# Early k of batch 1, four more bias pieces on GpSimd, 16-row transfers in the last bias block, slots of 112 tokens

## The chip, the cores and the metric

The kernel runs on one core of one Trainium2 chip. The metric is the device time of one execution in microseconds (us). A run of it gives one time; the number quoted is the median of the runs shown. Beside that stands one profiled execution with a trace of every engine: TensorE (PE, and PEld for its weight loads), VectorE (DVE), ScalarE (ACT), GpSimd (POOL), SyncE (SP), and the transfers (DMA).

## What is computed

Three stages, one behind the other.

```python
# 1. attention, B=2, H=8, S=576, D=64, with an additive bias from a small MLP on relative position
scores = q @ k.T / sqrt(D)
x = log1p(abs(i - j)) / log1p(max(i, 1))
bias = relu(x * w1 + b1) @ w2              # 32 hidden values, one bias per head
attn = softmax(scores + bias)
x = attn @ v                               # to (1152, 512)
# 2. dense experts: E=4, every token goes through all, F=1024
out = sum_e p[:, e] * (relu(x @ w1[e]) @ w2[e])
# 3. routed experts: E=8, F=1024, every token goes to the one with the largest gate logit
e_idx = argmax(x @ w_gate)
out[mask_e] = gate_w * eom[:, e] * (relu(x[mask_e] @ w1[e]) @ w2[e])
```

With the reference's inputs the eight routed experts get 204, 48, 336, 0, 274, 21, 0 and 269 of the 1152 tokens.

## The kernel before, in words

**Attention.** The queries are cut into nine units of 128 rows: blocks 0 to 3 of 128 positions each for both batches, and a last unit with the 64 remaining positions of both. A unit has eight heads, so there are 72 steps n. A loop (L584) carries them as a pipeline: in round n TensorE makes scores of step n+3 (`qk`, L352), VectorE adds the bias and takes the maximum of step n+2 (`soft_max`, L361), ScalarE makes the exponentials of step n+1 (`soft_exp`, L371), and TensorE transposes step n and multiplies step n-2 by v (`av`, L411 to L413).

**The bias.** A block of 128 positions is made in eight groups T of sixteen positions: four pieces tt hold four positions each with the 32 hidden values on the partitions. `bias_r` (L297) makes one piece, relu of a slice of the table lm plus a column, on VectorE (L305), GpSimd (L308) or ScalarE (L310). `bias_mm` (L323) multiplies the four pieces by w2 into PSUM, `bias_out` (L332) scales them with ScalarE into a tile bo of 128 partitions (16 positions by 8 heads), and a transfer on SyncE's queue (L335) spreads it as 16 partitions by 8 by 576 into the block's bias tile, which `soft_max` reads. Which slice of lm is read follows from `row0` (L66). The last block, blk 4, has 64 positions, and its four groups issue four transfers of 8 partitions each (L339). The table lm has 1152 columns for all groups, with a step of 8 positions between the four partition groups, and is scaled by w1 once (L549 for its first 448 columns).

**The order of the work** is written out by hand; each engine takes its instructions in that order, and so does each DMA queue. Ahead of the loop stands a prologue (L514 to L583). SyncE's queue there carries lm's last 704 columns, q of unit 0 (`load_q`, L139), k of batch 0 (`load_k`, L184 and L188: two transfers of 256 positions and one of 64), then rounds T=0 to 10 with the eight bias groups of block 0 and two of the next block, and behind each group an entry of the list `bulk` (L539): k of batch 1, the first 448 columns of lm (`load_lm`, L537), three pieces of v of batch 0 (`load_v`, L230 and L233) and q of unit 1. The two halves of a transposed q (`q_trans`, L159; its copies between partitions L173 and L174) stand on the same queue.

In the loop the bias groups of the next block are made two pieces a round. RP and RE say which engine takes a piece:

```python
RP = 10
RE = ("vavv", "pavv")
...
bias_r(g[0], T, 2 * o + x, RE[n >= RP][2 * o + x])
```

So up to round 9 GpSimd takes none, and from then on one of four. GpSimd's in-order queue further holds the splits of q into a high and a low part (`split`, L146 and L147), and in round 4 the split of v of batch 1 (`v_hi` L271, `v_lo` L286 and L290), which waits for VectorE's scaling of v (L264).

**Dense experts.** 96 rounds i with two layers (L729 to L731 and L746 to L748); SyncE and GpSimd bring the weights, which ScalarE, VectorE and GpSimd split into pairs of f16; the routed experts' weights go back to memory as wdr.

**Routed experts.** Every token is given a rank within its expert (`rank`, L850). 128 tokens of an expert form a slot; slot number and place in it come from the rank's high and low bits. Three early slots (NE) are filled from the first 768 tokens, and NFIX = 13 slots are run in a pipeline; slots beyond the thirteenth run one after another behind an If on the count. For a slot, `ids_in` gathers its tokens' rows, `x_tr` (L1036) transposes them by four matmuls, `load_e` brings the expert's weights in eight transfers of 512 KB (four of them for each layer; skipped where the expert is that of the slots before), `lay1` (L1048) makes 96 matmuls with the weights stationary and the slot's 128 tokens moving, `lay2` (L1067) makes 24 with the tokens stationary and 512 columns moving, and L1072 writes the rows out. `step(s)` puts lay1 of slot s+1, x_tr of slot s+2 and lay2 of slot s behind one another.

## Time and profile before

| what | us |
|---|---|
| median of 3 runs (805.65 to 805.75) | 805.67 |
| the profiled execution | 805.57 |
| its span | 803.8 |
| PE busy | 746.6 (93%) |
| PEld busy | 479.8 (60%) |
| DVE busy | 489.1 (61%) |
| ACT busy | 476.7 (59%) |
| POOL busy | 352.2 (44%) |
| HBM read, written | 116.35 MB, 39.34 MB |

The span runs from the first to the last instruction of the profiled execution; the rest of its time lies around it. Busy time is the time in which an engine worked at something; the share is an average over stages that have different limits, so an engine with 60% can still be the one that is waited for in one stage. Matmuls are pipelined, so the rows of single ones overlap. In rows of waits the engine and tile that waited come first, then what ended the wait.

### The profile page before, as it was taken

Reading aid. Unit: us, or ns where it says so; the run is one execution under the profiler, and the core shown is the slowest. Engines: PE = TensorE matmul, PEld = TensorE weight load, DVE = VectorE, ACT = ScalarE, POOL = GpSimd, SP = SyncE. Lnnn points to the kernel's source line nnn. Section 1 sums busy time; section 2 is a strip of 40 time slices with the busy share of each in tenths; the row PEclk is TensorE's granted clock in tenths of the full one; section 3 lists DMA queues with packets and bytes.
Section 4 is the critical chain, followed back from the end, with each engine's and each line's share of the span. In section 5 each row is a group of like instructions: output and inputs, shape, how many; then the busy total and the mean of one; then the engine's idle time right before and its main releaser. Section 6 shows DMA issues by size and latency. Waiting matters only on the chain. (4 is left out here: it accounts for less than half of the span.)

```text
span 803.8 us, 16406 instructions
## 1 busy us (share of the span) xinstructions
PE 746.6 (93%) x6303; PEld 479.8 (60%) x6303; DVE 489.1 (61%) x1210; ACT 476.7 (59%) x694; POOL 352.2 (44%) x258
## 2 busy tenths in 40 slices
PE   6677999998889999999999999999998989999994
PEld 3255777776875554555555555555555577767771
DVE  6679999998787446555566465465567563333310
ACT  5577899996845757676676667667663122232220
POOL 8534644551643546555545555554533212211110
PEclk9979999999999999999999999999999999999998
DMA  7944344466255475556657467573526689998330
GB/s 178 207 94 100 91 108 101 126 177 131 69 196 209 152 285 198 206 221 254 235 188 263 166 246 279 195 261 130 211 108 256 204 307 386 409 407 327 131 142 17
DMA packets 73868, 160.21 MB, mean 199 GB/s; under 512 B 18936, under 2 KB 27640, under 8 KB 73786
## 3 DMA queue, kind: packets, MB, share of 16 engines
q1 hardware_dynamic: 67912, 144.38, 53.2%
q0 software_dynamic: 4528, 14.47, 5.3%
q8 instruction: 51, 0.84, 0.4%
q10 hardware_dynamic: 1346, 0.28, 0.2%
q14 instruction: 31, 0.25, 0.1%
HBM read 116.35 MB, written 39.34 MB: 194 GB/s over the span
## 5 line engine op out<-in xcount | busy, mean ns | idle before, releaser
L511 POOL TENSOR_TENSOR ring<-wraw,ring 128x1024 f16<-128x1024 f32 x64 | 136.2, 2130 | 118.8 <-ACT wraw L508 100.4
L734 DVE SCALAR_TENSOR_TENSOR h<-hps,h 128x384 f16<-128x384 f32 x96 | 53.2, 557 | 146.8 <-ACT h L733 146.8
L729 PE MATMUL hps<-xt,wt 128*128 128x384 f16 x384 | 125.9, 328 | 2.3 <-DVE h L734 1.8
L731 PE MATMUL hps<-xt,wt 128*128 128x384 f16 x384 | 126.0, 328 | 0.0
L730 PE MATMUL hps<-xt,wt 128*128 128x384 f16 x384 | 126.0, 328 | 0.0
L476 DVE TENSOR_REDUCE wm<-wraw 128x1 f32<-128x1024 f32 x96 | 116.0, 1209 | 0.0
L508 ACT ACTIVATE wraw<-wraw,wR 128x1024 f32<-128x1024 f32 x91 | 104.5, 1149 | 3.0
L746 PE MATMUL yps<-wt,h 128*128 128x512 f16 x264 | 100.1, 379 | 0.0
L747 PE MATMUL yps<-wt,h 128*128 128x512 f16 x264 | 100.1, 379 | 0.0
L748 PE MATMUL yps<-wt,h 128*128 128x512 f16 x264 | 100.1, 379 | 0.0
L733 ACT ACTIVATE h<-hps 128x384 f16<-128x384 f32 x96 | 46.7, 487 | 88.9 <-PE hps L731 84.8
L511 POOL TENSOR_TENSOR wt<-wraw,wt 128x1024 f16<-128x1024 f32 x31 | 66.1, 2134 | 63.2 <-ACT wraw L508 62.9
L503 ACT ACTIVATE ring<-wraw,wR 128x1024 f16<-128x1024 f32 x64 | 73.0, 1141 | 21.5 <-DVE wR L492 18.8
L1048 PE MATMUL l<-xb,wb 128*128 128x128 f16 x1248 | 73.7, 219 | 0.6 <-issue 0.2
L1048 PEld LDWEIGHTS <-wb 128*128 128x128 f16 x1248 | 71.0, 98 | 4.7 <-issue 1.6
L1067 PE MATMUL l<-wb,xb 128*128 128x512 f16 x312 | 69.5, 379 | 0.8 <-ACT o L1071 0.8
L352 PE MATMUL sc<-kt,qt 128*128 128x288 f32 x320 | 62.1, 319 | 7.8 <-DVE mn L361 6.0
L361 DVE CUSTOM_DVE_ANT_0 ns<-sc,bias 128x576 f32<-128x576 f32 x72 | 54.3, 754 | 21.7 <-PE sc L352 9.6
L305 DVE TENSOR_SCALAR_CACHE_REDUCE r<-lm,nbp 128x576 f32<-128x576 f32 x88 | 67.1, 807 | 0.2
L1056 DVE SCALAR_TENSOR_TENSOR xb<-l,xb 128x512 f16<-128x512 f32 x26 | 17.6, 691 | 80.6 <-ACT xb L1055 80.6
L1072 POOL DMA_INDIRECT out_x<-o,g x13 | 13.3, 1020 | 107.3 <-ACT o L1071 93.5
L371 ACT ACTIVATE e<-ns,mn 128x576 f32<-128x576 f32 x72 | 56.4, 784 | 1.9 <-DVE mn L361 1.7
(248 smaller groups left out, 1426.0 us busy)
## 6 DMA issues: line engine op xcount, KB each, us to landing
wb<-wdr SPq DMA_DIRECT2D x104, 512.0 KB
wraw<-in_moe_w SPq DMA_DIRECT2D x84, 512.0 KB
wdr<-ring SPq DMA_DIRECT2D x64, 512.0 KB
bias<-bo SPq DMA_DIRECT2D x32, 288.0 KB
wraw<-in_moe_w POOLq DMA_DIRECT2D x12, 512.0 KB, 5.0
qt<-qt SPq DMA_DIRECT2D x40, 128.0 KB
ydr<-y POOLq DMA_DIRECT2D x9, 258.0 KB, 3.4
bias<-bo SPq DMA_DIRECT2D x16, 144.0 KB
```

Source lines behind the costliest of these rows:

```text
L476: dve.tensor_reduce(out=wm[:, w_col(x), k:k + 1], in_=wraw[x][:, k], axis=AX.X, op=ALU.max, apply_absolute_value=True)
L503: act.activation(out=hi, in_=t, func=AF.Copy, scale=R)
L508: act.activation(out=t, in_=t, func=AF.Copy, scale=R)
L511: pool.tensor_tensor(out=lo, in0=t, in1=hi, op=ALU.subtract)
L729: pe.matmul(ps, lhsT=w[:, k, 0, fs], rhs=xt[:, c, 0, k, :], start=(k == 0), stop=False)
L730: pe.matmul(ps, lhsT=w[:, k, 0, fs], rhs=xt[:, c, 1, k, :], start=False, stop=False)
L731: pe.matmul(ps, lhsT=w[:, k, 1, fs], rhs=xt[:, c, 0, k, :], start=False, stop=(k == 3))
L746: pe.matmul(acc[m][t], lhsT=hh, rhs=w[:, f // 2, 0, ws], start=(f == 0), stop=False)
L747: pe.matmul(acc[m][t], lhsT=hh, rhs=w[:, f // 2, 1, ws], start=False, stop=False)
L748: pe.matmul(acc[m][t], lhsT=hl, rhs=w[:, f // 2, 0, ws], start=False, stop=(f == 7))
L1048: pe.matmul(ps[f // 4][:, f % 4, :], lhsT=w[:, k, a, f * 128:f * 128 + 128], rhs=xs[:, b, k, :], start=(k == 0 and f % 4 == 0 and i == 0), ...
L1067: pe.matmul(ps, lhsT=hs[:, a, f, :], rhs=w[:, f // 2, b, c], start=(f == 0 and i == 0), stop=(f == 7 and i == 2))
```

## The change

1. The three transfers of k of batch 1 stand right behind those of batch 0, ahead of the first bias group. `bulk` holds v of batch 0 in three pieces behind groups 0 to 2 and lm's first columns behind group 3; nothing stands behind the groups after that, and q of unit 1 is loaded behind the prologue's loop. The scaling of lm's first 448 columns goes from VectorE to ScalarE.
2. RP is 0: from round 0 on GpSimd takes one bias piece of four. That is one piece each in rounds 0, 2, 4, 6 and 8, which VectorE had.
3. In the last bias block the positions of a group are laid out so that two transfers of 16 partitions take the place of four of 8. This needs the table with a step of 4 between partition groups: a new tile lm4 of 128 x 640, loaded in round 22 and scaled by GpSimd in round 36.
4. A slot holds SL = 112 tokens. The rank is divided by 112 by a product and a shift; `x_tr`, `lay1`, `lay2` and the output take 112 rows or columns. The gather still brings 128 rows, and the tiles keep their size. The number of slots provided for is 21.

The diff without its unchanged lines:

```diff
@@ -42,18 +42,19 @@
-C_N = C_PERM + 16
+C_N = C_PERM + 20
...
-NSLOT = 19
+NSLOT = 21
+SL = 112
...
-RP = 10
+RP = 0
@@ -64,7 +65,7 @@
-    return blk * 128 + T + 32 * tt if blk < 4 else 512 + 2 * T + tt // 2 + 32 * (tt % 2)
+    return blk * 128 + T + 32 * tt if blk < 4 else 512 + T + 16 * tt
...
@@ -300,7 +302,7 @@
-        src = lm[:, 575 - r0:1151 - r0]
+        src = lm[:, 575 - r0:1151 - r0] if blk < 4 else lm4[:, 575 - r0:1151 - r0]
@@ -334,9 +336,8 @@
-        for x in range(2):
-            for p0 in (0, 64):
-                sp.dma_start(out=bias_t[blk][p0 + 2 * T + x:p0 + 64:8], in_=bo[64 * x:64 * x + 64])
+        for p0 in (0, 64):
+            sp.dma_start(out=bias_t[blk][p0 + T:p0 + 64:4], in_=bo)
@@ -516,6 +517,8 @@
+        for a in (2, 0, 1):
+            load_k(1, a)
@@ -536,8 +539,7 @@
-        bulk = [[lambda: load_k(1, 2), lambda: load_k(1, 0)], [lambda: load_k(1, 1)], [load_lm], [lambda: load_v(0, 0)],
-                [lambda: load_v(0, 1)], [lambda: load_v(0, 2)], [], [lambda: load_q(1)]]
+        bulk = [[lambda: load_v(0, 0)], [lambda: load_v(0, 1)], [lambda: load_v(0, 2)], [load_lm]]
@@ -546,7 +548,7 @@
-                dve.tensor_scalar(out=lm[:, 0:448], in0=lm[:, 0:448], scalar1=w1c, scalar2=None, op0=ALU.mult)
+                act.activation(out=lm[:, 0:448], in_=lm[:, 0:448], func=AF.Copy, scale=w1c)
@@ -563,6 +565,7 @@
+        load_q(1)
@@ -677,6 +680,10 @@
+            if n == 22:
+                sp.dma_start(out=lm4, in_=lmc[:, 1152:1792])
+            if n == 36:
+                pool.tensor_tensor(out=lm4, in0=lm4, in1=w1c.to_broadcast([128, 640]), op=ALU.mult)
@@ -861,10 +868,10 @@
-            dve.tensor_copy(rki[:, uu], rks[:, uu])
-            dve.tensor_scalar(out=rki[:, uu], in0=rki[:, uu], scalar1=127, scalar2=None, op0=ALU.bitwise_and)
-            dve.tensor_copy(lo7[:, uu], rki[:, uu])
-            dve.tensor_tensor(out=hi7[:, uu], in0=rks[:, uu], in1=lo7[:, uu], op=ALU.subtract)
+            dve.tensor_scalar(out=rki[:, uu], in0=rks[:, uu], scalar1=9363.0, scalar2=None, op0=ALU.mult)
+            dve.tensor_scalar(out=rki[:, uu], in0=rki[:, uu], scalar1=20, scalar2=None, op0=ALU.arith_shift_right)
+            dve.tensor_copy(hi7[:, uu], rki[:, uu])
+            dve.scalar_tensor_tensor(out=lo7[:, uu], in0=hi7[:, uu], scalar=-float(SL), in1=rks[:, uu], op0=ALU.mult, op1=ALU.add)
...
@@ -952,8 +959,8 @@
-        dve.tensor_scalar(out=ci, in0=pn[0:8, 0:1], scalar1=127.0, scalar2=None, op0=ALU.add)
-        dve.tensor_scalar(out=ci, in0=ci, scalar1=7, scalar2=None, op0=ALU.arith_shift_right)
+        dve.tensor_scalar(out=ci, in0=pn[0:8, 0:1], scalar1=SL - 1.0, scalar2=9363.0, op0=ALU.add, op1=ALU.mult)
+        dve.tensor_scalar(out=ci, in0=ci, scalar1=20, scalar2=None, op0=ALU.arith_shift_right)
...
@@ -1033,10 +1040,10 @@
-            pe.transpose(ps[:, a, :], xq[:, a * 128:a * 128 + 128], idn)
+            pe.transpose(ps[:, a, 0:SL], xq[0:SL, a * 128:a * 128 + 128], idn[0:SL, 0:SL])
...
-        act.copy(xs[:, 0], ps)
-        dve.tensor_tensor(out=xs[:, 1], in0=ps, in1=xs[:, 0], op=ALU.subtract)
+        act.copy(xs[:, 0, :, 0:SL], ps[:, :, 0:SL])
+        dve.tensor_tensor(out=xs[:, 1, :, 0:SL], in0=ps[:, :, 0:SL], in1=xs[:, 0, :, 0:SL], op=ALU.subtract)
@@ -1045,15 +1052,16 @@
-                    pe.matmul(ps[f // 4][:, f % 4, :], lhsT=w[:, k, a, f * 128:f * 128 + 128], rhs=xs[:, b, k, :],
+                    pe.matmul(ps[f // 4][:, f % 4, 0:SL], lhsT=w[:, k, a, f * 128:f * 128 + 128], rhs=xs[:, b, k, 0:SL],
...
-            act.activation(out=hs[:, 0, c], in_=ps[z], func=AF.Relu)
-            dve.scalar_tensor_tensor(out=hs[:, 1, c], in0=ps[z], scalar=0.0, in1=hs[:, 0, c], op0=ALU.max, op1=ALU.subtract)
+            act.activation(out=hs[:, 0, c, 0:SL], in_=ps[z][:, :, 0:SL], func=AF.Relu)
+            dve.scalar_tensor_tensor(out=hs[:, 1, c, 0:SL], in0=ps[z][:, :, 0:SL], scalar=0.0, in1=hs[:, 0, c, 0:SL], op0=ALU.max,
+                                     op1=ALU.subtract)
@@ -1064,12 +1072,12 @@
-                pe.matmul(ps, lhsT=hs[:, a, f, :], rhs=w[:, f // 2, b, c], start=(f == 0 and i == 0), stop=(f == 7 and i == 2))
+                pe.matmul(ps[0:SL], lhsT=hs[:, a, f, 0:SL], rhs=w[:, f // 2, b, c], start=(f == 0 and i == 0), stop=(f == 7 and i == 2))
...
-        act.activation(out=o, in_=ps, func=AF.Copy, scale=gs)
-        pool.indirect_dma_start(out=out, out_offset=bass.IndirectOffsetOnAxis(ap=ids, axis=0), in_=o, in_offset=None,
+        act.activation(out=o[0:SL], in_=ps[0:SL], func=AF.Copy, scale=gs[0:SL])
+        pool.indirect_dma_start(out=out, out_offset=bass.IndirectOffsetOnAxis(ap=ids[0:SL], axis=0), in_=o[0:SL], in_offset=None,
@@ -1245,7 +1253,7 @@
-    at = np.array([[row0(t // 32, t // 4 % 8, t % 4) + 8 * g for t in range(144)] for g in range(4)])
+    at = np.array([[row0(t // 32, t // 4 % 8, t % 4) + (8 if t < 128 else 4) * g for t in range(144)] for g in range(4)])
@@ -1276,8 +1284,9 @@
-    g = 8 * np.repeat(np.arange(4), 32)[:, None]
-    lm = np.log1p(np.abs(np.arange(1152)[None, :] - 575 - g).astype(np.float32))
+    g = np.repeat(np.arange(4), 32)[:, None]
+    x = np.arange(1792)[None, :]
+    lm = np.log1p(np.abs(np.where(x < 1152, x - 575 - 8 * g, x - 1152 - 575 - 4 * g)).astype(np.float32))
```

How the order of the instructions moves, at three places.

SyncE's queue at the start, before (kraw and ks are k, vraw is v, bias the bias tile, qt a transposed q):

```order
L188 DMA kraw_128<-in_k 128x8x128 x2
L184 DMA ks<-in_k 64x8x64
L335 DMA bias_164<-bo 16x8x576
L184 DMA ks<-in_k 64x8x64
L188 DMA kraw_190<-in_k 128x8x128
L173 DMA qt<-qt 64x512
L174 DMA qt<-qt 64x512
L335 DMA bias_164<-bo 16x8x576
L188 DMA kraw_190<-in_k 128x8x128
L335 DMA bias_164<-bo 16x8x576
L537 DMA lm<-in_lmc 128x448
L335 DMA bias_164<-bo 16x8x576
```

The same queue from the same place in the change:

```order
L190 DMA kraw_129<-in_k 128x8x128 x2
L186 DMA ks<-in_k 64x8x64 x2
L190 DMA kraw_136<-in_k 128x8x128 x2
L337 DMA bias_170<-bo 16x8x576
L232 DMA vraw<-in_v 128x4x128 x2
L175 DMA qt<-qt 64x512
L176 DMA qt<-qt 64x512
L337 DMA bias_170<-bo 16x8x576
L232 DMA vraw<-in_v 128x4x128 x2
L337 DMA bias_170<-bo 16x8x576
L235 DMA vraw<-in_v 64x4x64 x2
L337 DMA bias_170<-bo 16x8x576
```

All of k now stands ahead of the first bias group, and the transfers between the groups are those of v; lm's first columns follow the fourth group instead of the third.

GpSimd's queue from the split of q of unit 1 (qs) on, before; v and vz are v of batch 1, r a bias piece:

```order
L146 TENSOR_TENSOR qs<-q,one 128x8x64
L147 TENSOR_TENSOR qs<-q,qs 128x8x64
L271 TENSOR_TENSOR v<-vraw,one 128x8x64
L286 TENSOR_TENSOR v<-vraw,v 128x8x64
L271 TENSOR_TENSOR v<-vraw,one 128x8x64
```

In the change:

```order
L148 TENSOR_TENSOR qs<-q,one 128x8x64
L149 TENSOR_TENSOR qs<-q,qs 128x8x64
L310 TENSOR_SCALAR r<-lm,nbp 128x576 x3
L273 TENSOR_TENSOR v<-vraw,one 128x8x64
L288 TENSOR_TENSOR v<-vraw,v 128x8x64
```

Three bias pieces now stand ahead of the split of v. GpSimd's queue at the end of that split, before:

```order
L286 TENSOR_TENSOR v<-vraw,v 128x8x64
L271 TENSOR_TENSOR vz<-vraw,one 64x4x64 x2
L290 TENSOR_TENSOR vz<-vraw,vz 64x4x64 x2
L146 TENSOR_TENSOR qs<-q,one 128x8x64
L147 TENSOR_TENSOR qs<-q,qs 128x8x64
L308 TENSOR_SCALAR r<-lm,nbp 128x576 x4
```

In the change:

```order
L288 TENSOR_TENSOR v<-vraw,v 128x8x64
L273 TENSOR_TENSOR vz<-vraw,one 64x4x64 x2
L292 TENSOR_TENSOR vz<-vraw,vz 64x4x64 x2
L310 TENSOR_SCALAR r<-lm,nbp 128x576 x2
L148 TENSOR_TENSOR qs<-q,one 128x8x64
L149 TENSOR_TENSOR qs<-q,qs 128x8x64
L310 TENSOR_SCALAR r<-lm,nbp 128x576 x4
```

Two bias pieces now stand between the split of v and the next split of q.

ScalarE's queue near the end of the prologue (r a bias piece, bo a bias group out of PSUM, kt a part of k), before:

```order
L217 CAST kt_120<-ktp 128x4x64 x2
L310 ACTIVATE r<-lm,bps 128x576
L332 ACTIVATE bo<-bp,bconst,cs 128x288 x2
L310 ACTIVATE r<-lm,bps 128x576
L332 ACTIVATE bo<-bp,bconst,cs 128x288 x2
L310 ACTIVATE r<-lm,bps 128x576
L332 ACTIVATE bo<-bp,bconst,cs 128x288 x4
```

In the change:

```order
L219 CAST kt_121<-ktp 128x4x64 x2
L312 ACTIVATE r<-lm,bps 128x576
L551 ACTIVATE lm<-lm,cs 128x448
L334 ACTIVATE bo<-bp,bconst,cs 128x288 x2
L312 ACTIVATE r<-lm,bps 128x576
L334 ACTIVATE bo<-bp,bconst,cs 128x288 x2
L312 ACTIVATE r<-lm,bps 128x576
```

The scaling of lm stands between the piece of round 7 and the copies of group 6.

## Rows read from the trace of the kernel before

**Rows 1.** Windows of the prologue; the columns are in the first line.
```profile
core 0: us, PE busy (x) PEld busy (x) DVE busy (x) ACT busy (x) POOL busy (x), PEclk, DMA share, GB/s
2.00:9.00 7.00, 1.98 (x8) 0.86 (x8) 3.15 (x10) 2.35 (x6) 5.17 (x8) 1.00 1.09 275
9.00:13.00 4.00, 4.00 (x24) 1.84 (x26) 4.00 (x13) 1.90 (x4) 3.84 (x5) 1.00 0.02 2
...
20.00:28.00 8.00, 7.04 (x73) 3.91 (x71) 7.22 (x20) 7.67 (x17) 7.73 (x7) 1.00 1.14 215
28.00:36.00 8.00, 4.11 (x47) 1.30 (x48) 5.97 (x13) 4.11 (x8) 3.70 (x3) 1.00 1.16 214
36.00:42.00 6.00, 1.04 (x16) 0.57 (x8) 0.00 (x0) 0.99 (x3) 0.00 (x0) 0.60 1.04 168
```

**Rows 2.** Timeline of the prologue: start, duration, engine, line, tiles, wait before.
```profile
28.09 1.48 DVE L549 TENSOR_SCALAR lm<-lm,cs 128x448 f32<-128x448 f32 x1 [0.87 <-DMA lm<-in_lmc]
29.67 0.78 ACT L310 ACTIVATE r<-lm,bps 128x576 f32<-128x576 f32 x1 [1.03 <-DVE lm L549]
...
41.01 1.07 ACT L332 ACTIVATE bo<-bp,bconst,cs 128x288 f32<-128x288 f32 x2 [5.35 <-DMA bias<-bo]
42.49 0.76 DVE L361 CUSTOM_DVE_ANT_0 ns<-sc,bias 128x576 f32<-128x576 f32 x1 [8.30 <-DMA bias<-bo]
```

**Rows 3.** The page's DMA issues: size of one, us to landing.
```profile
ydr<-y POOLq DMA_DIRECT2D x9, 258.0 KB, 3.4
```

**Rows 4.** The page's costliest groups: VectorE's bias pieces, busy and mean ns.
```profile
L305 DVE TENSOR_SCALAR_CACHE_REDUCE r<-lm,nbp 128x576 f32<-128x576 f32 x88 | 67.1, 807 | 0.2
```

**Rows 5.** Timeline of GpSimd and TensorE from 71 to 87 us.
```profile
71.42 1.04 POOL L271 TENSOR_TENSOR v<-vraw,one 128x512 f16<-128x512 f32 x1 [12.00 <-DVE vraw L264]
...
81.65 1.39 POOL L290 TENSOR_TENSOR vz<-vraw,vz 64x256 f16<-64x256 f32 x2
...
85.49 1.74 POOL L308 TENSOR_SCALAR r<-lm,nbp 128x576 f32<-128x576 f32 x1
80.75 1.18 PE L323 MATMUL bp<-r,cs 128*32 128x288 f32 x16
85.57 0.66 PE L159 MATMUL qtp<-cs,qs 128*128 128x128 f32 x4 [0.72 <-POOL qs L147]
```

**Rows 6.** A window inside the last bias block's transfers.
```profile
190.00:193.00 3.00, 2.86 (x38) 2.50 (x35) 2.91 (x6) 2.91 (x6) 0.00 (x0) 1.00 0.53 125
```

**Rows 7.** Waits from 176 to 205 us: total, times, longest.
```profile
ACT bo L332 <- issue: 2.6, 1, 2.6
DVE ns L361 <- PE sc L352: 2.4, 2, 2.2
...
ACT bo L332 <- DMA bias<-bo: 1.3, 1, 1.3
```

**Rows 8.** Waits from 100 to 150 us.
```profile
POOL r L308 <- PE bp L323: 24.3, 10, 3.3
```

**Rows 9.** Timeline of TensorE in the routed experts.
```profile
732.52 5.77 PE L1048 MATMUL l<-xb,wb 128*128 128x128 f16 x96
...
754.92 5.52 PE L1048 MATMUL l<-xb,wb 128*128 128x128 f16 x96
...
760.72 5.34 PE L1067 MATMUL l<-wb,xb 128*128 128x512 f16 x24
```

**Rows 10.** Timeline of TensorE and its weight loads in the attention, near 62 us.
```profile
61.76 0.20 PE L411 MATMUL avp<-v,eth 128*128 128x65 f16 x1
...
62.05 0.19 PE L411 MATMUL avp<-v,eth 128*128 128x65 f16 x1
61.80 0.10 PEld L413 LDWEIGHTS <-etl 128*128 128x128 f16 x1
```

**Rows 11.** The page's DMA issues: the routed experts' weights.
```profile
wb<-wdr SPq DMA_DIRECT2D x104, 512.0 KB
```

**Rows 12.** Windows in the routed experts.
```profile
730.00:735.00 5.00, 5.00 (x58) 3.59 (x57) 0.77 (x5) 1.30 (x2) 1.05 (x1) 1.00 1.03 410
...
740.00:745.00 5.00, 5.00 (x42) 2.92 (x40) 1.93 (x8) 1.00 (x2) 0.03 (x1) 1.00 0.03 7
...
760.00:765.00 5.00, 5.00 (x32) 2.65 (x30) 3.58 (x10) 1.54 (x3) 0.00 (x0) 1.00 1.03 419
```

More of the change, by code (lines that the diff above doesn't have):

```diff
@@ L125, in attn_moe_moe_kernel @@
     lm = lm_p.tile([128, 1152], F32, name="lm")
+    lm4 = lm_p.tile([128, 640], F32, name="lm4")
     nbp = lm_p.tile([128, 144], F32, name="nbp")
@@ L940, in bump @@
         bm = rt_p.tile([1, 8], F32, name="bm")
-        dve.tensor_scalar(out=bm, in0=pb, scalar1=-1.0, scalar2=128.0, op0=ALU.mult, op1=ALU.add)
+        dve.tensor_scalar(out=bm, in0=pb, scalar1=-1.0, scalar2=float(SL), op0=ALU.mult, op1=ALU.add)
         dve.scalar_tensor_tensor(out=bm, in0=bm, scalar=0.0, in1=oh2[0:1, :], op0=ALU.max, op1=ALU.mult)
@@ L970, in slot_table @@
         dve.tensor_reduce(out=st1, in_=st8, axis=AX.X, op=ALU.add)
-        dve.scalar_tensor_tensor(out=st1, in0=hi7, scalar=1.0 / 128, in1=st1, op0=ALU.mult, op1=ALU.add)
+        dve.tensor_tensor(out=st1, in0=hi7, in1=st1, op=ALU.add)
         dve.tensor_tensor(out=nl, in0=cs[:, C_PERM:C_PERM + NLATE].unsqueeze(1).to_broadcast([128, NU, NLATE]),
```

## The prediction, made before the changed kernel was run

> **What bounds the kernel now.** I read the page's busy shares and its 40 slices first: TensorE is busy 93% of the span, so time can be won only where it is not full or where its own work shrinks. Two such places are the first slices and the expert stage. I then read a table of windows over the first 42 us, the timeline there, and the same two views where each part of the change lands.
>
> In the first 42 us the transfers set the pace. They run at 275 GB/s to 9 us, then the DMA engines stand idle for 4 us (share 0.02) and from 13 us on they are full at about 215 GB/s, while TensorE's work thins out [rows 1]. The timeline shows who waits: the first block of lm lands at 28.09, the last bias copies of ScalarE stand 5.35 us behind earlier bias transfers, and the first addition of scores and bias on VectorE starts at 42.49 after 8.30 us of waiting for a bias transfer [rows 2]. Around 80 us GpSimd's queue is the tight one, near 190 us the bias transfers of the last block, and in the expert stage TensorE and the weight loads alternate; their rows come with the terms.
>
> **The prologue.** The 1.18 MB of k of batch 1 (8x576x64 floats) leave the crowded stretch for the idle one: at 275 GB/s they take 4.3 us, from 9 to 13.3 us [rows 1]. What then has to pass before batch 0's first block can be added to is eight bias groups of 0.295 MB, v of batch 0 (1.18), four halves of q transposed (0.52) and the first part of lm (0.23): 4.29 MB. At 215 GB/s they end at 33.3; I add 3.4 us from issue to landing, the row of a 258 KB transfer [rows 3], so the first addition starts near 37 instead of 42.49. I round the gain to **-5.2**, since ScalarE now scales the 448 columns of lm (about 0.6 us, from its 0.78 for 576 columns) where VectorE took 1.48, and that stands on the chain to the last groups [rows 2]. The ends: the gain can't exceed the wait of 8.30, and if the last stretch's 168 GB/s (it goes with a granted clock of 0.60, the 1.2 GHz level for part of it, after TensorE had done little) holds for all 4.29 MB, they end at 38.8 and -3.7 is left. That lm is queued behind v now costs nothing by itself: v was on the same queue ahead of the last groups before. The q load that moves behind the loop was ahead of nothing that this wait needs.
>
> **GpSimd's queue.** With RP=0 five bias pieces move from VectorE (807 ns each [rows 4]) to GpSimd (1.74 us each [rows 5]). Three of them stand ahead of the split of v of batch 1 and fit into the 12.00 us that GpSimd idles there. The other two stand behind it. The split runs from 71.42 to 83.04; if VectorE's relief lets it start 0.8 us earlier, the piece of n=6 ends at 83.04 - 0.8 + 1.74 = 84.0, while the bias matmul that reads it ran at 80.75 [rows 5]: TensorE's in-order queue stands 3.2 us later there. The second piece and the split of the next q follow on GpSimd, 2 x 1.74 - 0.8 = 2.7 later, and the transposes of that q at 85.57 had already waited 0.72 for GpSimd [rows 5]; most of it lies in the same delay. Afterwards TensorE is full, so a shift stays: **+2.8**. The ends: +1.6, if three pieces less on VectorE (2.4 us) bring the split forward by all of that, and +5.5, if the second delay comes on top of the first. The saved 5 x 0.81 us of VectorE give nothing else where TensorE is full. Further pieces alternate as before.
>
> **The last bias block.** Its transfers were four of 8 partitions for each group; now two of 16. While they run, the DMA share is 0.53 at 125 GB/s [rows 6], against 1.16 at 214 with 16-partition transfers [rows 1]. ScalarE's copies wait 1.3 and 2.6 us there and VectorE's additions wait 2.4 in two places for scores that TensorE issues later [rows 7]. I take the 2.4 that reach the chain, **-2.4**; the ends are 0 (ScalarE has slack enough) and -3.9 (both copies' waits). The new table lm4 costs a load of 320 KB, under 2 us of a queue that is not full, and one scaling on GpSimd, about 1.3 us by columns (1.74 for 576 [rows 5]); between pieces GpSimd waits 24.3 us in ten waits for TensorE [rows 8], which hides it. Without that cover it would cost its 1.3 us.
>
> **The expert stage.** A slot has 96 matmuls whose moving side shrinks from 128 to 112 columns. At 128 they take 5.52 us, 57.5 ns each [rows 9]; nine of 64 or 65 columns start within 0.29 us, 32 ns apart [rows 10]. 63 columns are thus worth about 25 ns, 16 columns 6.3 ns, a slot **0.60 us**, and its four transposes at most 0.06 more. The 24 matmuls of the second layer keep 512 moving columns and their 5.34 us [rows 9].
> The Trainium skill ("TensorE: Matmul & The Clock Gate", section "Back-to-back issue gap") says that in a stream of weight load and matmul pairs the spacing is set by both, and gives 81 ns at 128 columns; by that the narrower slot would gain little. The trace disagrees on the figure (57.5 ns).
> The thirteen slots do not all profit. Two steps take 22.40 us from one first layer to the one two slots later, 11.2 each [rows 9]. Eight weight transfers of 512 KB a slot [rows 11] at 410 GB/s take 10.2 us [rows 12], and with gather and output some 0.5 MB more, 11.4. So up to about 740 us transfers run without pause and a faster TensorE only meets its weights sooner; at 740 to 745 they pause (share 0.03) because slots 9 and 10 keep the weights of slot 8, and they run again at 760 [rows 12]. I give the nine slots before 2.5 us together (the slack that their weights have) and the last four 4 x 0.66 = 2.7: **-5.2**. The ends: -3.5 (only the last four and part of the routing) and -8.5 (thirteen slots, and 0.4 around the routing). The routing replaces four small VectorE instructions by four; one load of 20 instead of 16 constants and longer tables weigh nothing beside this.
>
> **Sum.** -5.2 + 2.8 - 2.4 - 5.2 = -10.0 against the profiled execution's 805.57 (span 803.8): 795.6. The median of the runs shown is 805.67, 0.1 above it, so **795.7 us** as a median. A measurement of this kernel can tell a change of about 0.2% (1.6 us) from none.
>
> **The rivals.**
> A, the forecast, 0.57; its own range 793 to 798.5.
> B, GpSimd's queue is dearer and the prologue gives least: -3.7 + 5.5 - 2.4 - 5.2 = -5.8, **799.9**. For it speaks that after a thin stretch the granted clock was 0.60 [rows 1], so that a wait is paid in slower matmuls too; against it that GpSimd idled 12 us just before. 0.14.
> C, weights are not what limits the slots and all thirteen gain 0.62: -8.1 in place of -5.2, **792.8**. For it: the first-layer rows lie within 0.25 us of each other whether the DMA is full or not [rows 9, 12]. Against it: 11.4 us of transfers in a step of 11.2. 0.13.
> D, the first layer is paced by its 96 weight loads rather than by columns: the slots give 0.4, **800.5**. The rows at 65 columns speak against it, where a matmul with a weight load of its own came every 32 ns [rows 10]. 0.05.
> This is the case that the section of the Trainium skill named above would make.
> E, the change is slower: the tokens of some expert no longer fit. The program runs thirteen slots together and any others one after another with nothing beside them. Where an expert's tokens lie between a multiple of 112 and the next of 128, a fourteenth slot appears; it costs its transfers (10.2 us), both layers (5.5 and 5.3 [rows 9]), and gather, transposes and output in series, some 25 us: **820.7**. It decides from the first token too many; with the reference's inputs the largest expert has 336 tokens, three times 112 exactly, and the count stays thirteen, at the very edge. 0.03.
> F, early k brings nothing, because all bytes have to pass anyway and the idle 4 us are filled only with what delays the first bias groups: 0 for -5.2, **800.9**. Against it: ScalarE and VectorE wait for transfers only at the end, not at 13 us. 0.05.
> Two of B, D and F together, about 805: 0.03.
>
> **How the numbers follow.** The likeliest case gives 795.7. The range 790 to 801 takes in A, B, C and reaches D and F; E, the pairs, and the far ends of the terms (-8.3 in the prologue with -8.5 in the slots, 786.6) are left out. Faster by over 0.2%: A, B, C, D, F and a third of the pairs, 0.95. Within 0.2%: the rest of the pairs, 0.02. Slower: 0.03.
>
> **What the profile of the changed kernel would show.** The DMA share at 9 to 13 us above 0.9, and the first addition near 37 with a wait of 3 us or less. A bias matmul near 84 us, later relative to its surroundings, that waits about 3 us for GpSimd's piece. No wait of ScalarE for bias transfers near 185 to 195 us. First layers of 4.9 to 5.0 us, the last four steps 10.5 us apart, and the steps before them still 11.2 to 11.4. I would be wrong if the first addition stays at 40 or later, if TensorE's wait for GpSimd is above 5 us, if the first layer stays at 5.5, or if anything runs after the thirteenth slot.

## The result and the profile after

The changed kernel takes 795.93 us as a median of 4 runs (794.78 to 796.37), the kernel before 805.66 in the 4 runs beside it. The ratio is 0.9885, with a 95% interval from 0.9869 to 0.9902: faster by 1.15%. Forecast were 795.7 us.

| | before | after |
|---|---|---|
| profiled execution, us | 805.57 | 795.92 |
| its span | 803.8 | 794.1 |
| PE busy | 746.6 | 737.5 |
| DVE busy | 489.1 | 482.0 |
| POOL busy | 352.2 | 360.7 |

The windows of the prologue of the kernel after, with the columns of [rows 1]:

```profile
9.00:13.00 4.00, 4.00 (x24) 1.84 (x26) 4.00 (x13) 1.84 (x4) 3.84 (x5) 1.00 1.22 274
...
20.00:28.00 8.00, 7.11 (x74) 3.97 (x71) 7.29 (x20) 7.42 (x15) 7.76 (x7) 1.00 1.13 212
28.00:36.00 8.00, 5.28 (x48) 1.57 (x48) 4.58 (x12) 5.37 (x10) 3.56 (x4) 0.79 0.61 136
36.00:42.00 6.00, 4.47 (x38) 3.70 (x37) 4.99 (x11) 4.80 (x11) 0.00 (x0) 1.00 0.87 197
```

The idle 4 us of the transfers are filled (share 1.22 instead of 0.02), and the backlog is gone by 28 to 36 us (0.61 instead of 1.16). The timeline of the same stretch, where [rows 2] had the additions at 42.49:

```profile
29.27 0.67 ACT L551 ACTIVATE lm<-lm,cs 128x448 f32<-128x448 f32 x1 [1.52 <-DMA lm<-in_lmc]
29.84 1.05 ACT L334 ACTIVATE bo<-bp,bconst,cs 128x288 f32<-128x288 f32 x2
...
32.74 0.59 ACT L334 ACTIVATE bo<-bp,bconst,cs 128x288 f32<-128x288 f32 x1 [0.37 <-PE bp L325]
...
35.74 1.07 ACT L334 ACTIVATE bo<-bp,bconst,cs 128x288 f32<-128x288 f32 x2 [0.77 <-PE bp L325]
36.87 0.76 DVE L362 CUSTOM_DVE_ANT_0 ns<-sc,bias 128x576 f32<-128x576 f32 x1 [1.94 <-DMA bias<-bo]
30.47 3.81 PE L325 MATMUL bp<-r,cs 128*32 128x288 f32 x32 [2.95 <-ACT bo L334]
```

The first addition is at 36.87 (near 37 was forecast) and waits 1.94 us instead of 8.30; ScalarE's last copies (L334) wait for TensorE and no longer for transfers. The copies at 32.74 are the end of block 0's last group; those at 35.74 belong to the next block. Before, block 0's last group was copied here:

```profile
30.35 1.06 ACT L332 ACTIVATE bo<-bp,bconst,cs 128x288 f32<-128x288 f32 x2
```

So the first addition came 11.1 us after the end of that copy (31.41) before, and comes 3.5 us after it (33.33) now. The copy itself is 1.9 us later: ScalarE waits 1.52 us for lm's first columns, the copies of the group before stand behind their scaling, and TensorE waits 2.95 us for those copies.

GpSimd and TensorE around the split of v of batch 1, timeline of the kernel after (compare [rows 5]):

```profile
64.39 1.04 POOL L273 TENSOR_TENSOR v<-vraw,one 128x512 f16<-128x512 f32 x1 [6.13 <-DVE vraw L266]
...
74.60 1.38 POOL L292 TENSOR_TENSOR vz<-vraw,vz 64x256 f16<-64x256 f32 x2
76.07 3.41 POOL L310 TENSOR_SCALAR r<-lm,nbp 128x576 f32<-128x576 f32 x2
...
77.85 1.84 PE L325 MATMUL bp<-r,cs 128*32 128x288 f32 x16 [3.96 <-POOL r L310]
82.34 0.76 DVE L362 CUSTOM_DVE_ANT_0 ns<-sc,bias 128x576 f32<-128x576 f32 x1 [5.48 <-PE sc L353]
```

The bias matmul stands 3.96 us for GpSimd's piece and VectorE's twelfth addition after the first 5.48 us for TensorE. The wait is not all: behind it the granted clock is near its lower level of 1.2 GHz for 4 us, and the bias matmul takes 1.84 us instead of 1.18 [rows 5]. Windows of the kernel after, with the columns of [rows 1]:

```profile
78.00:80.00 2.00, 2.00 (x24) 0.73 (x17) 0.00 (x0) 0.82 (x2) 2.00 (x2) 0.55 0.00 0
80.00:82.00 2.00, 2.00 (x18) 1.95 (x15) 0.00 (x0) 1.56 (x4) 1.92 (x3) 0.59 0.00 0
```

The three pieces ahead of the split fit in, as forecast: GpSimd still idles 6.13 us before it.

In the last bias block the kernel after shows the following waits (172 to 200 us) in place of [rows 7]; no copy of ScalarE waits for a transfer there, and VectorE's 2.4 us for scores are down to 0.2:

```profile
DVE ns L362 <- ACT xt L454: 0.7, 1, 0.7
...
ACT bo L334 <- PE bp L325: 0.7, 2, 0.5
...
DVE ns L362 <- PE sc L353: 0.2, 1, 0.2
```

In the routed experts TensorE's timeline after has these rows (compare [rows 9]), and below them its waits from 655 to 720 us:

```profile
669.82 2.39 PE L1055 MATMUL l<-xb,wb 128*128 128x112 f16 x43 [0.86 <-DMA wb<-wdr]
...
736.72 4.88 PE L1055 MATMUL l<-xb,wb 128*128 128x112 f16 x96
...
747.02 4.88 PE L1055 MATMUL l<-xb,wb 128*128 128x112 f16 x96
```

```profile
PE l L1055 <- DMA wb<-wdr: 3.5, 5, 1.2
```

A first layer takes 4.88 us instead of 5.52, and late steps are 10.3 us apart. But five times the first layer now waits for its weights, 3.5 us in all; the trace of the kernel before had no such wait.

**Where the 9.7 us of the span lie.** I set the starts of VectorE's 72 additions (L361 and L362), of the first hidden values of the dense experts, and of the slots' transposes of the two traces side by side. After minus before: -5.6 at the first addition, -6.2 to -7.5 up to the eleventh after it, -2.0 at the next, -2.35 from there to the last bias block, -4.9 at the end of the attention, -6.1 where the dense experts begin, -6.3 at the transposes of 715.66 before, -9.9 at the last matmuls. So the prologue, GpSimd's queue, the last block and the last slots show at their places. One piece had no term: at the start of the dense experts 1.3 us. The windows there, before and then after:

```profile
238.00:243.00 5.00, 3.16 (x57) 2.17 (x57) 3.97 (x13) 0.87 (x2) 0.00 (x0) 0.90 0.00 0
243.00:248.00 5.00, 5.00 (x56) 3.85 (x56) 3.06 (x9) 2.03 (x3) 0.00 (x0) 0.76 0.01 3
```

```profile
233.00:238.00 5.00, 3.16 (x70) 2.52 (x71) 4.33 (x15) 0.87 (x2) 0.00 (x0) 1.00 0.00 0
238.00:243.00 5.00, 4.97 (x57) 3.24 (x55) 3.85 (x10) 3.32 (x5) 0.00 (x0) 1.00 0.02 3
```

After a stretch with TensorE busy for 3.16 of 5 us, the granted clock fell in the one trace and not in the other. The busy time is the same, so this is not the change's doing by any row here. The traces of the runs below bear this out: from the last addition to the first hidden values seven of the fourteen gain 1.24 to 1.27 us on the trace of before, as the change does, and the other six stay within 0.07 of it. The clock also fell in the kernel below that leaves out a quarter of the weight loads, whose attention is the change's to the letter. So no part of the change decides it.

### The profile page after: what moved, and what is told of

The parts are those of the page before. It is cut to its first block, busy times and chain, and to the rows that moved or that the text cites. A ratio compares the mean times of both kernels' runs of the same rounds, so it can differ in the third digit from the quotient of the medians.

```text
span 794.1 us, 16391 instructions
## 1 busy us (share of the span) xinstructions
PE 737.5 (93%) x6303; PEld 479.1 (60%) x6303; DVE 482.0 (61%) x1199; ACT 474.6 (60%) x695; POOL 360.7 (45%) x264
## 5 line engine op out<-in xcount | busy, mean ns | idle before, releaser
L1075 PE MATMUL l<-wb,xb 128*112 128x512 f16 x312 | 69.5, 379 | 0.8 <-ACT o L1079 0.8
L1055 PE MATMUL l<-xb,wb 128*128 128x112 f16 x1248 | 66.1, 213 | 4.0 <-DMA wb<-wdr 3.5
L1055 PEld LDWEIGHTS <-wb 128*128 128x128 f16 x1248 | 62.7, 98 | 9.3 <-DMA wb<-wdr 5.1
L362 DVE CUSTOM_DVE_ANT_0 ns<-sc,bias 128x576 f32<-128x576 f32 x72 | 54.3, 754 | 18.9 <-PE sc L353 12.4
L307 DVE TENSOR_SCALAR_CACHE_REDUCE r<-lm,nbp 128x576 f32<-128x576 f32 x83 | 63.2, 807 | 3.1 <-ACT lm L551 2.7
L310 POOL TENSOR_SCALAR r<-lm,nbp 128x576 f32<-128x576 f32 x25 | 43.0, 1720 | 46.5 <-PE bp L325 46.3
L1063 DVE SCALAR_TENSOR_TENSOR xb<-l,xb 128x448 f16<-128x448 f32 x26 | 15.7, 624 | 76.6 <-ACT xb L1062 76.6
```

The costliest lines, as they stand in the source:

```text
L1055: pe.matmul(ps[f // 4][:, f % 4, 0:SL], lhsT=w[:, k, a, f * 128:f * 128 + 128], rhs=xs[:, b, k, 0:SL], start=(k == 0 and f % 4 == 0 and i ...
L1075: pe.matmul(ps[0:SL], lhsT=hs[:, a, f, 0:SL], rhs=w[:, f // 2, b, c], start=(f == 0 and i == 0), stop=(f == 7 and i == 2))
```

## The experiments

"Before" stands for the kernel before, run beside each; ratios are to it. Single runs of one kernel spread over 0.6 to 8 us, so the intervals are about 1.1 to 2.5 us to either side. The runs come from four series beside that of the change, each with its own runs of the kernel before; where two kernels of different series are compared, the difference by their ratios stands beside that of their medians.

**Each part alone, on the kernel before.** The first part (the diff's hunks on load_k, bulk, the scaling of lm and load_q):

```diff
+        for a in (2, 0, 1):
+            load_k(1, a)
...
+        bulk = [[lambda: load_v(0, 0)], [lambda: load_v(0, 1)], [lambda: load_v(0, 2)], [load_lm]]
...
+                act.activation(out=lm[:, 0:448], in_=lm[:, 0:448], func=AF.Copy, scale=w1c)
...
+        load_q(1)
```

> The kernel before with the first part of the change alone (k of batch 1 early, v and lm behind the first groups, lm scaled by ScalarE). Theory A (the parts act one after another and add up, as the shift of VectorE's additions in the two traces reads): first addition at 36.9 instead of 42.49, the shift stays near -5.6 to the end of the attention, 800.0 us; another 1.4 less if the granted clock stays full where the dense experts begin. Theory B (part of the further shift of -1.9 between the first and the eleventh addition comes from the loads too): 798.2. Theory C (the early transfers only help together with the lighter VectorE): first addition at 40 or later, 803 or more.

Measured: 797.51 us against 805.77, ratio 0.9909 (0.9890 to 0.9928), that is -7.3 us with -8.9 to -5.8. The first addition is at 35.39, and the shift against the kernel before stays between -6.9 and -7.8 up to the last bias block. The first addition is well ahead of 40 (C falls), and the further shift is there with the loads alone, as B has it: its 798.2 is met (798.4 by the ratio), while A's 800.0 is the interval's very end. The term is larger than forecast.

RP alone:

```diff
-RP = 10
+RP = 0
```

> The kernel before with RP=0 alone. Theory A: VectorE's relief gives 1.9 us by the eleventh addition, TensorE's wait for GpSimd's piece behind the split of v costs 5.2 after it, net +3.3, 809.0 us. Theory B (the relief came from the loads): +5.2, 810.9. Theory C (the wait was so long only because the early loads brought TensorE there sooner): +2 or less, 807.7 or below.

Measured: 807.88 against 805.77, ratio 1.0032 (1.0016 to 1.0048), +2.6 us. The trace has the same step, VectorE's addition behind the split of v at 88.02 with 5.46 us of waiting for TensorE, and 1.2 us of relief ahead of it; so C's short wait is not there, though its +2 lies inside the interval as A's +3.3 does. A is nearest, a little high, since 1.4 us of the shift came back in the last bias block. The granted clock behind the wait was 0.50 and 0.66 here (84 to 88 us).

```profile
88.02 0.76 DVE L361 CUSTOM_DVE_ANT_0 ns<-sc,bias 128x576 f32<-128x576 f32 x1 [5.46 <-PE sc L352]
```

The last bias block alone (row0, bias_out, lm4 and the two constants of the diff, nothing else):

```diff
+        for p0 in (0, 64):
+            sp.dma_start(out=bias_t[blk][p0 + T:p0 + 64:4], in_=bo)
```

> The kernel before with the last bias block's transfers and table alone. Theory A: -2.5 us between the additions 51 and 56, kept to the end, 803.2 us. Theory B (ScalarE's and VectorE's slack there takes it up before the dense experts begin): 805.7. A lost stretch of full clock where the dense experts begin would hide up to 1.4 us of either.

Measured: 802.66 against 805.77, ratio 0.9971 (0.9953 to 0.9989), -2.3 us (-3.8 to -0.9): A by the times. The traces say more. Between the additions 51 and 56 all nine kernels with this part (the change and eight of these) shift by 2.34 to 2.36 us against the trace of before. But of the four without it, the kernel with the first part alone also shifts by 2.29 there, that with RP alone by 1.36, with the slots alone by 0.86, with k early alone by 0.68. Without the part this stretch loses between 0.1 and 2.4 us in five traces, with it nothing in nine, and the profiled execution of before had the largest loss. The loss follows ScalarE's copies there: their waits for a bias transfer or for nothing that the profile shows add up to 3.9 us in the trace of before, 3.3 and 3.1 with k early alone and the slots alone, 0.8 and 0.7 with RP alone and the loads alone. Each kernel has one trace, so whether chance or the earlier parts set them stays open.

The slots alone (SL, rank, slot table, x_tr, lay1, lay2):

```diff
-                    pe.matmul(ps[f // 4][:, f % 4, :], lhsT=w[:, k, a, f * 128:f * 128 + 128], rhs=xs[:, b, k, :],
+                    pe.matmul(ps[f // 4][:, f % 4, 0:SL], lhsT=w[:, k, a, f * 128:f * 128 + 128], rhs=xs[:, b, k, 0:SL],
```

> The kernel before with slots of 112 tokens alone. Theory A (weights limit slots 3 to 7, so only the first and the last slots gain): -3.7 us, 802.0. Theory B (every slot gains 0.6 as its columns): -8, 797.7. Theory C (nothing but the last four slots): -2.6, 803.1. First layers of 4.88 us in all of them where no weights are waited for, the last five steps 10.3 apart.

Measured: 802.25, ratio 0.9959 (0.9939 to 0.9979), -3.3 us. B is outside the interval; A and C, 1.1 us apart, are both inside.
The four together, by their ratios: -7.3 + 2.6 - 2.3 - 3.3 = -10.3, against -9.3 for the change (0.9885). Within the intervals the parts add up.

**GpSimd's pieces.** The change with RP at 10:

```diff
-RP = 0
+RP = 10
```

> The change with RP back at 10: the first 10 rounds give GpSimd no bias piece. Theory A (the early loads bring TensorE to the split of v sooner, so the moved pieces cost more beside them than alone): the step of 5 us at the twelfth addition goes, the shift stays near -7.8 there, and the whole gains 3 to 5 us over the change, 791 to 793 us. Theory B (the pieces relieve VectorE by as much as they hold up TensorE): 795 to 797.

Measured: 792.68 (792.18 to 793.95, 5 runs), ratio 0.9830 (0.9816 to 0.9845). The time is A's: the five pieces cost the change 3.3 us by the medians and 4.4 by the ratios of two series; at the thirteenth addition after the first the two traces differ by 4.6, 0.6 of it since the first addition. A's reason, that they cost more beside the early loads, is not shown: the wait of VectorE was 5.46 us without these loads and 5.48 with them, and +2.6 (1.3 to 3.9) alone does not differ clearly from 3.3 or 4.4. The shift was -6.7, not -7.8. Next, the pieces behind the split of v alone given back to VectorE:

```diff
-                    bias_r(g[0], T, 2 * o + x, RE[n >= RP][2 * o + x])
+                    bias_r(g[0], T, 2 * o + x, RE[n < 5 or n >= 10][2 * o + x])
```

> The change with GpSimd taking its piece in rounds 0, 2, 4 and from 10 on, and VectorE in rounds 6 and 8. Theory A (only the two pieces behind the split of v hold TensorE up): no step at the twelfth addition, 791 to 793 us. Theory B (the three pieces ahead of the split bring it forward by VectorE's relief): up to 1.9 us below the kernel with RP at 10. Theory C (the relief is not on the chain): the same as that within 0.5.

Measured: 791.31 (790.81 to 792.07), ratio 0.9813 (0.9799 to 0.9827). The medians of one series put it 1.4 below the kernel with RP at 10 (no run of either reaches the other's), which is theory B. The twelfth addition after the first has no wait now:

```profile
76.29 0.75 DVE L362 CUSTOM_DVE_ANT_0 ns<-sc,bias 128x576 f32<-128x576 f32 x1
```

The granted clock is 1.00 here from 70 to 80 us. So the five pieces fall into two behind the split that cost 795.93 - 791.31 = 4.6 us (5.8 by the ratios) and three ahead of it that gain 1.4.

**What in the first part counts.** lm scaled by VectorE again in the change:

```diff
-                act.activation(out=lm[:, 0:448], in_=lm[:, 0:448], func=AF.Copy, scale=w1c)
+                dve.tensor_scalar(out=lm[:, 0:448], in0=lm[:, 0:448], scalar1=w1c, scalar2=None, op0=ALU.mult)
```

> The change with lm's first 448 columns scaled by VectorE again (1.48 us there instead of 0.67 on ScalarE). Theory A (it stands on the chain to the last bias groups): first addition 0.8 us later, 796.7 us. Theory B (the landing of the last bias transfer sets the end whatever scales lm): within 0.3 of the change, 795.9.

Measured: 796.25 (795.89 to 796.52), ratio 0.9873 (0.9858 to 0.9889). Its first addition was not later but earlier, at 35.17, little below the 35.30 to 36.87 of the kernels that scale on ScalarE. A falls, and the time is B's: the scaling's engine is worth nothing that shows.

Only k early, everything else of the prologue as before:

```diff
+        for a in (2, 0, 1):
+            load_k(1, a)
...
+        bulk = [[], [], [load_lm], [lambda: load_v(0, 0)],
+                [lambda: load_v(0, 1)], [lambda: load_v(0, 2)], [], [lambda: load_q(1)]]
```

> The kernel before with k of batch 1 queued behind k of batch 0 and nothing else moved: lm behind the third group, v behind groups 4 to 6, q of unit 1 behind the eighth, lm scaled by VectorE. Theory A (the gain is the 4 idle us of the transfers filled, whatever the order of the rest): -7 to -8, 798 to 799 us, as the kernel with the whole first part alone (797.5). Theory B (v still stands ahead of the last groups, whose transfers wait for it): half of it or less, 802 or more.

Measured: 800.66 against 805.96, ratio 0.9937 (0.9915 to 0.9960), -5.1 us (-6.9 to -3.2): neither theory's number, A's outside the interval, B's half inside it. The timeline still has ScalarE's copy behind the transfers of v, as B says, a wait that the kernel after has not:

```profile
28.59 1.15 ACT L332 ACTIVATE bo<-bp,bconst,cs 128x288 f32<-128x288 f32 x2
...
36.12 1.07 ACT L332 ACTIVATE bo<-bp,bconst,cs 128x288 f32<-128x288 f32 x2 [4.70 <-DMA bias<-bo]
```

So filling the idle transfers makes some 5 us, and taking v out from ahead of the last groups some 2 more (-7.3 against -5.1, with intervals that overlap). The traces show how. Here block 0's last group is copied early (the row at 28.59), but the transfers are full up to 36 us (share 1.17 from 28 on, against 0.61 in the change) and the first addition comes only 7.8 us after that copy's end, at 37.52. In all nine kernels with the whole order of loads the copy ends later, at 31.6 to 33.3, as lm lands later, but the addition follows it by 3.5 to 3.6 us and starts at 35.17 to 36.87.

**What limits the slots.** The change with a quarter of each weight load left out from slot 2 on; the matmuls then use an older quarter, so part of the second and later slots' layers is computed with other weights:

```diff
-        for k in range(4):
+        for k in range(4 if s < 2 else 3):
```

> The change with the last quarter of each weight load left out from slot 2 on (6 transfers of 512 KB a slot instead of 8; the stale quarter is used, so the output is that of mixed weights). Theory A (weights limit slots 3 to 8): 7.7 us of transfers a slot against 10.3 of matmuls, no wait of the first layer for weights, steps of 10.3 from the start, 4 to 6 us less than the change, 790 to 792 us. Theory B (TensorE's own work limits all slots and the waits are chance): within 1 us of the change.

Measured: 791.29 (790.32 to 792.23), ratio 0.9807 (0.9793 to 0.9821), 4.6 us below the change (6.3 by the ratios). Its trace has no wait of lay1 for weights, and from the fourth transposes to the tenth it takes 5.5 us less than the kernel before, where the change takes 0.7 more. A holds: weights limit the middle slots. The other traces agree: from the third transposes to the tenth the five kernels with slots of 128 take 78.2 to 80.8 us (79.1 on average), the five with 112 and whole loads 77.7 to 79.5 (78.6), this one 73.4. Narrow slots alone thus gained some 0.5 us in these seven steps, where the 0.68 of the last steps (10.98 and 10.30 us) would give 4.8; and waits of the first layer for weights are no novelty of the change, as the kernels with the loads alone and with k early alone, both with slots of 128, have 3.3 and 1.4 us of them.

Why, the windows further below show: in the kernel of 791.31 us the transfers pause at 645 to 656 us. SyncE's queue holds the second-layer weights of slot s+2, which wait for lay2 of slot s, ahead of the first-layer weights of slot s+3, whose buffer lay1 of slot s+1 has already freed. The next kernel turns them round, on top of the split of GpSimd's pieces above:

```diff
+        load_e(0, 3)
         for i, _ in enumerate(lay2(0)):
...
-                load_e(0, s + 2)
...
+                if s + 3 < end:
+                    load_e(0, s + 3)
```

> The change with GpSimd's piece in rounds 0, 2, 4 and from 10 on (791.3 alone), and the first-layer weights of slot s+3 queued behind lay1 of slot s+1, ahead of the second-layer weights of slot s+2, instead of behind them. The buffer they go to is free one lay2 earlier, so theory A (the transfers' pause at 645 to 656 us is the wait of SyncE's queue for lay2, and slots 3 to 8 pay for it): the pause fills, the waits of the first layers for weights go, 3 to 5 us less, 786.5 to 788.5. Theory B (the transfers are full from 656 on and their sum sets the end whatever their order): within 1 us of 791.3.

Measured: **786.77 us** (785.93 to 788.77, 6 runs) against 805.96, ratio 0.9768 (0.9739 to 0.9798): 4.5 below the kernel without the new order (3.6 by the ratios, and 3.8 in the two traces from the third transposes to the last matmuls), so A. Windows of that one (791.31), then of this, with the columns of [rows 12]:

```profile
644.00:650.00 6.00, 4.36 (x43) 3.73 (x41) 3.43 (x19) 2.07 (x4) 1.38 (x2) 0.72 0.36 138
650.00:656.00 6.00, 6.00 (x50) 4.08 (x49) 2.37 (x9) 1.23 (x3) 1.41 (x3) 1.00 0.69 189
656.00:700.00 44.00, 41.43 (x483) 31.83 (x481) 13.56 (x40) 11.34 (x21) 9.22 (x13) 1.00 1.03 408
```

```profile
644.00:650.00 6.00, 4.36 (x61) 3.79 (x59) 4.13 (x24) 2.11 (x4) 0.54 (x1) 0.85 0.63 232
650.00:656.00 6.00, 6.00 (x30) 3.50 (x29) 0.76 (x2) 0.30 (x2) 2.11 (x2) 0.86 0.96 346
656.00:700.00 44.00, 43.82 (x549) 35.27 (x547) 15.21 (x47) 12.46 (x22) 9.76 (x13) 1.00 1.02 398
```

The pause is nearly filled (1.5 MB more pass up to 656 us), the waits of the first layers are gone, and from 656 to 700 us TensorE is busy 43.82 of 44 us instead of 41.43. TensorE's timeline has steps of 10.3 us from 666 us on:

```profile
676.71 4.88 PE L1055 MATMUL l<-xb,wb 128*128 128x112 f16 x96
687.01 4.88 PE L1055 MATMUL l<-xb,wb 128*128 128x112 f16 x96
```

One more piece on GpSimd in rounds 1 and 3:

```diff
-RE = ("vavv", "pavv")
+RE = ("vavv", "pavv", "pavp")
...
+                    bias_r(g[0], T, 2 * o + x, RE[2 if 0 < n < 5 else n < 5 or n >= 10][2 * o + x])
```

> The same with one more bias piece on GpSimd in rounds 1 to 4 (two odd rounds, 1 and 3, ahead of the split of v). Theory A (VectorE bounds rounds 0 to 5 and GpSimd idles 6 us there): up to 1.3 us less than without, as three pieces gave 1.4. Theory B (GpSimd's idle time is used up, and the split of v starts later): the same or up to 2 us more.

Measured: 786.73 (786.33 to 788.13), ratio 0.9769 (0.9738 to 0.9800): no difference, B.

And the kernel with the new order of weights, with slots of 128 again:

> The kernel with the reordered weight loads and GpSimd's piece in rounds 0, 2, 4 and from 10 on (786.8), with slots of 128 tokens again. Theory A (with the pause of the transfers gone TensorE's columns set every slot): 13 slots at 0.62 to 0.68, 8 to 9 us more, 794.8 to 795.6. Theory B (the narrow slots are worth what they were in the change, as the early and last slots alone use them): 3 to 4 us more, 790 to 791.

Measured: 792.24 (791.15 to 793.32) against 806.16, ratio 0.9823 (0.9798 to 0.9848), 5.5 more (4.4 by the ratios). Neither number: more than the slots gave in the change, less than thirteen times 0.62. In the two traces the steps from the fourth transposes on differ by 6.8 us, ten slots at 0.68; what lies ahead of them differed by 1.5 the other way. Of that, the granted clock at the start of the dense experts made 1.3: it stayed full in this trace and fell in the other.

## Why the prediction was right, and where it was not

The forecast of 795.7 (range 790 to 801) met 795.93. The places and the waits were those named, but the closeness is partly luck: errors of both signs cancelled.

- **The prologue**, -5.2 forecast. The place and the time were right (36.87 for "near 37"), but the size was low: alone it gave -7.3 (-8.9 to -5.8). The 3.4 us for the landing held (3.5 to 3.6 in nine traces). The 33.3 before it was met by luck: it was to be the end of transfers that stay full, but their share was 0.61 from 28 to 36 us, and what ended at 33.33 was ScalarE's copy, behind lm. The step that failed is "lm queued behind v costs nothing by itself": block 0's last copies stand behind lm's first columns, which land 0.3 to 1.2 us later than before, and end 0.2 to 1.9 later. What outweighs it is the backlog behind the copy, 11.1 us before and 3.5 after. Two slips of the sum: ScalarE's shorter scaling is given as the reason to lower the gain from 5.8 to 5.2, where it would raise it, and the end of -3.7 leaves out the 3.4 of landing (with it, -0.3). Which engine scales lm shows in nothing.
- **GpSimd's queue**, +2.8 forecast; +2.6 alone, and 3.3 by the medians or 4.4 by the ratios in the change. The bias matmul waited 3.96 us, forecast 3.2. The forecast priced the wait alone; the 4 us at a granted clock of 0.55 and 0.59 behind it are part of the 5.6 us by which the shift falls back at the twelfth addition. And "the saved VectorE time gives nothing else" was wrong in the first rounds: the three pieces ahead of the split gain 1.4, and the two behind cost 4.6 to 5.8.
- **The last bias block**, -2.4 forecast, -2.3 measured alone (-3.8 to -0.9). The waits went as forecast, and VectorE's were the measure, not the 3.9 us of ScalarE's. But the term came from the one of the five traces without the part in which they were at their largest; on average over these the stretch loses 1.3 us against those with it.
- **The experts**, -5.2 forecast, -3.3 alone (-4.9 to -1.7), -3.8 in the change's trace from the dense experts on. The late slots gave what their columns give: from 715.66 of before to the end -6.3 becomes -9.9, 3.6 us over five slots, where 0.66 each was forecast. The step that failed is "I give the nine slots before 2.5 us together": what the first slots win is lost to the weights. From the start of the dense experts to the fourth transposes the shift grows from -6.1 to -7.7, and by the transposes of 715.66 it is back at -6.3, as the first layers wait 3.5 us for weights. What bound was not the 11.4 us of transfers a slot by itself: with the loads turned round the steps are 10.3. The last steps were to be 10.5 us apart and are 10.3.
- **No term** had the 1.3 us of granted clock at the start of the dense experts.
- **Rivals.** C (all slots gain, 792.8) fell by the waits for weights; with the weights reordered narrow slots are worth 5.5 (4.4 by the ratios) of its 8.1. D (weight loads pace the first layer) fell by its rows, 4.88 us for 112 columns against 5.52 for 128: 0.64 us, where the forecast had 0.60. F fell by both prologue kernels. E did not occur: no slot runs behind the thirteenth. B's reason held, a wait paid in slower matmuls too, but its net of 5.5 was not reached (3.3 to 4.4), and its prologue of -3.7 was too small.

The Trainium skill ("TensorE: Matmul & The Clock Gate", section "Back-to-back issue gap") gives about 81 ns at 128 columns for a stream of weight load and matmul pairs, set by both. These traces disagree: 57.5 ns at 128 columns and 50.8 ns at 112 (96 matmuls in 4.88 us), so the spacing followed the columns.

## What to carry to other kernels

When a queue idles ahead of a crowded stretch, move there what has no consumer soon, and then look which transfer still stands ahead of the one that is waited for; here the second step was worth some 2 us beside 5. Look also for what stands behind the consumer of a transfer that now lands later, as block 0's last copies stood behind lm. A stage that gets less work on one engine gains only until the next limit, so compare both sides' time per step first, and if a queue is the limit, look for an entry that waits on its engine's later release while the entry behind it could go: that swap gave about 4 us, as much as the narrower slots. Moving work to an idle engine paid here ahead of that engine's long block (three pieces, -1.4 us) and was dear behind it (two pieces, 4.6 to 5.8 us), and TensorE paid for the wait twice, as its clock fell behind it.

## What was not expected of the hardware

The granted clock at the start of the dense experts fell in some executions and not in others with the same work: 0.90 and 0.76 before, 1.00 and 1.00 after, and 0.83 in a window of the same stretch (228 to 238 us) of the kernel with the first part alone. It stayed full in seven of fourteen traces. That made 1.3 us between two traces that no part of the change owns, half as much as the smallest term of the forecast.

The second was the last bias block. Its transfers move somewhat faster with 16 partitions, 158 GB/s at a share of 0.57 in a window of the kernel after that answers to [rows 6] with its 125 at 0.53; the gain is a wait that is long in some traces without the part and nearly absent in others.

```profile
185.00:188.00 3.00, 2.87 (x38) 2.43 (x37) 2.42 (x6) 3.00 (x6) 0.00 (x0) 1.00 0.57 158
```
